# One weight load is requested four steps later: behind the write of the tenth tile of tokens

## The chip, the cores and the metric

The kernel runs on one core of a Trainium2 chip. Its engines are TensorE (PE in the profile, with its weight loads as PEld), VectorE (DVE), ScalarE (ACT), GpSimd (POOL) and SyncE (SP), which here does nothing but issue transfers. All transfers of SP stand in one queue that 16 DMA engines serve; GpSimd's gathers and scatters stand in a queue of their own, on the same 16 engines. The metric is the device time of one execution in microseconds: 433.91 us is the median of three runs before the change (433.2 to 435.3).

## What is computed

Three stages on 2 x 768 = 1536 tokens of 512 numbers. First an attention with decaying state for 8 heads, then a gated feed-forward stage with a convolution along the sequence, and then a mixture of 8 experts in which each token goes to one expert:

```python
def _moe_ref(x, w_in, conv_w, w_out):
    h = np.maximum(x @ w_in, 0.0)
    ...
    return (h * gate @ w_out).astype(np.float32)

def _moe2_ref(x, w_gate, w_local, w1, w2):
    logits = np.einsum('bsd,de->bse', x, w_gate)
    ...
            fresh_e = int(np.argmax(logits[b, s]))
            if s == 0 or local_gate[b, s] < 0.5:
                e = fresh_e
            else:
                e = prev_e if prev_e >= 0 else fresh_e
            ...
            h = np.maximum(x[b, s] @ w1[e], 0.0)
            out[b, s] = p[e] * (h @ w2[e])
```

Everything is float32. The change touches only the passage from the second stage to the third.

## The kernel before, in words

The tokens are cut into 12 tiles of 128, six for each of the two sequences. For each tile, `ffn_out` multiplies the gated hidden values with `w_out` on TensorE (L133 to L135, three matmuls for each product, tile `x_ps`). ScalarE copies the finished tile to SBUF (L486) and SP writes it to a DRAM buffer `xs` (L488), 256 KB for each tile. Tiles 1 to 10 go through a buffer `xn`; the last two (`xl4`, `xl5`) stay in SBUF as well, because the first two expert tiles take their rows from there.

While the second sequence's tiles are made, routing on VectorE works out which token goes to which expert, and writes a table `ei` of experts (L619) and a table `it` of token numbers (L657).

The third stage works on 11 expert tiles of 128 tokens that share an expert, and on two groups of smaller quarter tiles. For expert tile j, `gather(j)` zeroes a buffer `xg` and lets GpSimd fetch the tile's tokens from `xs` by an indirect DMA (L724). The gathers of tiles 0 and 1 need the first ten writes to `xs`; their rows from the last two tiles are added on TensorE from SBUF (`begin_x`, `late_x`, L810 and L816). The third gather is that of the first quarter group (number 16). It and all later ones need all twelve writes. TensorE turns a gathered tile (L797, `tp<-cs,xg`) and then multiplies it with w1 (tile `g`) and w2 (tile `y`). ScalarE and VectorE cut the weights in a high and a low part first (`cut`, L714 and L715).

Weights come in 2 MB pieces, each as four transfers of 512 KB that SP issues: `fetch(j, which)` (L695, buffers `r`; which is 0 for w1 and 1 for w2) for expert tile j, and `fetch_q` (L705, buffers `qc` and `qs1l`) for the quarter groups. From the second expert tile on (`fetch(1, ...)`) SP reads the expert's number from `ei` before it issues (L676).

There is no scheduler: every engine executes its instructions in the order in which the code issues them. For the second sequence this order is set by the loop at L769. Its step n is one call of `ffn_out` (six matmuls), and the tiles are written at n = 2, 4, 8, 12, 16 and 20. Tables, weight requests and gathers are put in at given values of n; `experts` follows with `fetch(1, 1)`, `fetch_q(0, 0, 1)`, the turning of tiles 0 and 1, and gather 16.

Of the kernel before, what the change touches and what calls it, by code (L numbers as in the profile page):

```python
# [91 lines left out]
def tile_kernel(ctx, tc, cat, cst, qT, kT, kN, vN, w_in, conv_w, w_out, wg, w1, w2, out):  # L92
# [378 lines left out]
    def ffn_out(b, t, ms):  # L471

        ts = slice(t * P, (t + 1) * P)
        if ms[0] == 0:
            OUT[b, t] = psb.tile([P, DM], F32, tag="x2", name="x2_ps")
        ps = OUT[b, t]
        for m in ms:
            g = hg[b, m]
            mm3(ps, g[:, 0, ts], g[:, 1, ts], wo_hi[:, m, :], wo_lo[:, m, :], m == 0, m == 7)
        if ms[-1] == 7:  # L480
            if b == B - 1 and t >= NG - 2:
                xn = xpool[0].tile([P, DM], F32, name=f"xl{t}", bufs=1)
                LAST.append(xn)
            else:
                xn = rt.tile([P, DM], F32, name="xn", bufs=2)
            se.activation(out=xn, in_=OUT.pop((b, t)), func=AF.Copy)  # L486
            r = b * S + t * P
            sy.dma_start(out=xs[r:r + P, :], in_=xn)  # L488
# [194 lines left out]
    def fetch(j, which):  # L683

        src = (w1, w2)[which].rearrange("e p a n -> e p (a n)")
        kw = {}
        if j == 0:
            src = src[0]
        else:
            src = src[bass.ds(expert_at(j), 1)].rearrange("o p n -> (o p) n")  # L690
            if j > 1:
                kw = dict(cond=sy.value_load(ei[0:1, 1, j:j + 1], min_val=0, max_val=1), cond_hint=True)
        dst = raw(j % 2, which)
        for i in range(4):
            sy.dma_start(out=dst[:, i, :], in_=src[:, i * 1024:(i + 1) * 1024], **kw)  # L695

    def fetch_q(g, which, i):

        tag = QSLOT[nq[0] % 2]
        nq[0] += 1  # L700
        QW[g, which, i] = w = home(tag).tile([P, 4, 1024], F32, tag=tag, name="q" + tag)
        src = (w1, w2)[which].rearrange("e p a n -> e p (a n)")
        for u in range(4):
            one_e = src[bass.ds(expert_at(NTILE + 4 * g + u), 1)].rearrange("o p n -> (o p) n")
            sy.dma_start(out=w[:, u, :], in_=one_e[:, i * 1024:(i + 1) * 1024])  # L705

    def cut(j, which, i):

        tag = SLOT[ncut[0] % len(SLOT)]
        ncut[0] += 1  # L710
        w = home(tag).tile([P, 2, 2, 1024], F32R, tag=tag, name="w" + tag)
        for h in range(2):
            r = RAW[j % 2, which][:, 2 * i + h, :]
            se.activation(out=w[:, 0, h, :], in_=r, func=AF.Copy)  # L714
            ve.tensor_tensor(out=w[:, 1, h, :], in0=r, in1=w[:, 0, h, :].bitcast(F32), op=ALU.subtract)  # L715
        W[j, which, i] = w.rearrange("p s h n -> p s (h n)")
# [3 lines left out]
    def gather(j, n=NT):  # L720

        X[j] = xg = xpool[0].tile([P, DM], F32, name="xg")
        po.memset(xg, 0.0)
        return po.indirect_dma_start(out=xg, out_offset=None, in_=xs[0:n], in_offset=bass.IndirectOffsetOnAxis(ap=it[:, j:j + 1], axis=0),  # L724
                                     bounds_check=n - 1, oob_is_err=False)
# [43 lines left out]
    for n, (t, ms) in enumerate(units, 1):  # L769
        ffn_out(1, t, ms)  # L770
        for step in STEPS.get(n, ()):
            next(step, done)
        if n == 8:
            fetch(1, 0)
        if n in (10, 14):
            cut(0, 0, n // 14)
        if n == 13:
            fetch_q(0, 0, 0)
            for j in range(2):
                gather(j, NT - 2 * P)  # L780
# [279 lines left out]
```

## Time and profile before

| what | us |
|---|---|
| median of three runs (lowest to highest) | 433.91 (433.2 to 435.3) |
| the profiled execution | 433.53 |
| its span, first to last instruction | 431.8 |
| PE busy | 406.7 (94%) |
| DVE busy | 290.1 (67%) |
| ACT busy | 259.4 (60%) |

Times in the profile count from the start of the span, so that an event at 240.02 us is 240.02 us after the first instruction. The 1.7 us between the profiled execution and its span lie around the program. The profile gives the granted clock of TensorE as a share of full speed; it is 1.00 in all of the stretches shown below. An idle time in brackets behind an instruction is that of its engine just before it, with what ended it.

### The profile page before, as it was taken

To read this page: it belongs to the slowest core of one execution; us is meant where nothing else is said; L and a number is where in the kernel's file an instruction comes from. 1 tells how busy PE (TensorE), PEld (TensorE's weight loads), DVE (VectorE), ACT (ScalarE), POOL (GpSimd) and SP (SyncE) were. 2 spreads that over 40 slices of the span, in tenths; PEclk is the share of its full clock that TensorE was granted. 3 is DMA by queue.
4 is the path that set the end of the run, shared out by engine and by line. 5 is a ranking of instruction groups with operands and counts; after the bars stand their busy time and mean duration, and the time that the engine had idled before them with its cause. 6 is when DMAs were issued, how large, how long until landed. Compare 5 with 4: busy or idle time off the path is not lost.

```text
span 431.8 us, 7294 instructions
## 1 busy us (share of the span) xinstructions
PE 406.7 (94%) x2412; PEld 327.2 (76%) x2412; DVE 290.1 (67%) x518; ACT 259.4 (60%) x429; POOL 91.6 (21%) x92
## 2 busy tenths in 40 slices
PE   8898999997999999999999899999989999999991
PEld 7787897896898778989768676867738676776881
DVE  3798789798766350477899057968663796858650
ACT  2787677666755212566604166869555786958560
POOL 5256664213000000000000330205212132111210
PEclk9999999999999999999999999999999999999997
DMA  7989773320000101000296999999979999675001
GB/s 239 380 289 399 257 218 87 96 92 1 2 2 0 49 29 46 26 0 2 82 355 214 358 382 350 347 385 407 379 272 330 393 367 362 266 257 205 34 26 37
DMA packets 27324, 86.59 MB, mean 201 GB/s; under 512 B 3598, under 2 KB 4622, under 8 KB 27280
## 3 DMA queue, kind: packets, MB, share of 16 engines
q1 hardware_dynamic: 25200, 79.76, 50.6%
q0 software_dynamic: 2080, 6.29, 3.8%
q8 instruction: 21, 0.34, 0.3%
q14 instruction: 23, 0.19, 0.1%
HBM read 105.18 MB, written 6.55 MB: 259 GB/s over the span
## 4 chain that ended last, share of the span: by engine, by line
PE 35%; issue 26%; DMA 18%; DVE 14%; ACT 3%; POOL 2%; SPq 0%; POOLq 0%; DVEq 0%
DMA out_dram<-yo,it 15%; PE h_ps L133 5%; PE h_ps L135 4%; PE h_ps L134 4%; PE x_ps L133 4%; PE x_ps L134 3%; PE x_ps L135 3%; PE y L297 3%; PE s_ps L279 3%; DVE cc L350 2%; DMA kv<-in_kN_dram 2%; DVE na L149 2%; PE inc L287 2%; DVE na L150 1%; PE y L299 1%
## 5 line engine op out<-in xcount | busy, mean ns | idle before, releaser
L133 PE MATMUL h_ps<-xT,wih 128*128 128x384 f32 x128 | 46.5, 363 | 2.3 <-ACT wc L192 2.3
L350 DVE SCALAR_TENSOR_TENSOR cc<-h,cw,cc 128x768 f32<-128x768 f32 x32 | 35.1, 1097 | 16.8 <-ACT cc L347 16.8
L860 POOL DMA_INDIRECT out_dram<-yo,it x13 | 16.7, 1283 | 137.1 <-ACT yo L859 137.1
L724 POOL DMA_INDIRECT xg<-xs,it x13 | 18.8, 1442 | 125.5 <-DMA qc<-in_w_dram 118.6
L134 PE MATMUL h_ps<-xT,wih 128*128 128x384 f32 x128 | 43.1, 337 | 0.0
L135 PE MATMUL h_ps<-xT,wil 128*128 128x384 f32 x128 | 43.1, 336 | 0.0
L133 PE MATMUL x_ps<-woh,hg 128*128 128x512 f32 x96 | 38.5, 401 | 0.0
L134 PE MATMUL x_ps<-wol,hg 128*128 128x512 f32 x96 | 37.5, 391 | 0.0
L135 PE MATMUL x_ps<-woh,hg 128*128 128x512 f32 x96 | 37.5, 390 | 0.0
L715 DVE TENSOR_TENSOR ws0l<-r,ws0l 128x1024 fp32r<-128x1024 f32 x22 | 26.0, 1222 | 16.3 <-ACT ws0l L714 16.1
L297 PE MATMUL y<-at,vz 128*128 128x128 f32 x192 | 30.6, 281 | 1.7 <-DMA kv<-in_kN_dram 0.9
L715 DVE TENSOR_TENSOR ws0h<-r,ws0h 128x1024 fp32r<-128x1024 f32 x22 | 26.0, 1222 | 8.3 <-ACT ws0h L714 8.2
L715 DVE TENSOR_TENSOR wc<-r,wc 128x1024 fp32r<-128x1024 f32 x22 | 25.9, 1221 | 7.9 <-ACT wc L714 7.9
L714 ACT ACTIVATE ws0l<-r 128x1024 fp32r<-128x1024 f32 x22 | 22.1, 1052 | 13.6 <-PE y L135 13.6
L153 POOL TENSOR_TENSOR na<-na,raw 128x512 int32<-128x512 int32 (+1 forms) x17 | 21.9, 1290 | 38.2 <-DVE na L150 12.6
L715 DVE TENSOR_TENSOR ws1h<-r,ws1h 128x1024 fp32r<-128x1024 f32 x22 | 26.0, 1222 | 6.0 <-ACT ws1h L714 4.0
L279 PE MATMUL s_ps<-qz,kq 128*128 128x256 f32 x96 | 29.0, 384 | 1.0 <-DVE qz L248 1.0
L714 ACT ACTIVATE wc<-r 128x1024 fp32r<-128x1024 f32 x22 | 22.1, 1054 | 11.3 <-PE g L135 11.3
L297 PEld LDWEIGHTS y<-at,vz 128*128 128x128 f32 x192 | 25.3, 191 | 4.3 <-DVE xT L302 2.3
L133 PEld LDWEIGHTS h_ps<-xT,wih 128*128 128x128 f32 x128 | 24.1, 188 | 5.5 <-ACT wc L192 2.6
L281 DVE TENSOR_TENSOR at<-s_ps,ca 128x256 f32<-128x256 f32 x48 | 20.2, 420 | 11.6 <-PE s_ps L279 11.5
L486 ACT ACTIVATE xn<-x_ps 128x512 f32<-128x512 f32 x10 | 6.0, 599 | 32.8 <-PE x_ps L135 15.5
(231 smaller groups left out, 1041.5 us busy)
## 6 DMA issues: line engine op xcount, KB each, us to landing
r<-in_w_dram SPq DMA_DIRECT2D x88, 512.0 KB
qc<-in_w_dram SPq DMA_DIRECT2D x32, 512.0 KB
qs1l<-in_w_dram SPq DMA_DIRECT2D x32, 512.0 KB
raw<-in_w_in_dram SPq DMA_DIRECT2D x8, 512.0 KB
raw<-in_w_out_dram SPq DMA_DIRECT2D x8, 512.0 KB
kq<-in_qT_dram SPq DMA_DIRECT2D x7, 384.0 KB
kq<-in_kT_dram SPq DMA_DIRECT2D x7, 384.0 KB
kv<-in_vN_dram SPq DMA_DIRECT2D x7, 384.0 KB
```

The source lines that it names most:

```text
L133: te.matmul(ps, lhi, rhi, start=first, stop=False)
L134: te.matmul(ps, lhi, rlo, start=False, stop=False)
L135: te.matmul(ps, llo, rhi, start=False, stop=last)
L153: po.tensor_tensor(out=a, in0=a, in1=lo, op=ALU.add)
L279: te.matmul(ps, self.kq[:, 0, tok], self.qz[:, :, tok], start=True, stop=True)
L281: ve.tensor_tensor(out=self.at[c], in0=ps, in1=self.dm, op=ALU.mult)
L297: te.matmul(y, vz[:, c, j, :], at[:, j, :], start=(j == 0), stop=(c == 0 and j == 1))
L350: ve.scalar_tensor_tensor(out=cc, in0=h[:, i:i + S], scalar=cw[:, m, i:i + 1], in1=cc, op0=ALU.mult, op1=ALU.add)
L714: se.activation(out=w[:, 0, h, :], in_=r, func=AF.Copy)
L715: ve.tensor_tensor(out=w[:, 1, h, :], in0=r, in1=w[:, 0, h, :].bitcast(F32), op=ALU.subtract)
L724: return po.indirect_dma_start(out=xg, out_offset=None, in_=xs[0:n], in_offset=bass.IndirectOffsetOnAxis(ap=it[:, j:j + 1], axis=0), bound ...
L860: po.indirect_dma_start(out=out, out_offset=bass.IndirectOffsetOnAxis(ap=it[:, j:j + 1], axis=0), in_=yo, in_offset=None, bounds_check=NT ...
```

## The change

The request for w1 of the second expert tile (`fetch(1, 0)`, four transfers of 512 KB into buffer `r10`) moves from step n = 8 of the loop to n = 12.

```diff
         ffn_out(1, t, ms)
         for step in STEPS.get(n, ()):
             next(step, done)
-        if n == 8:
+        if n == 12:
             fetch(1, 0)
         if n in (10, 14):
             cut(0, 0, n // 14)
         if n == 13:
             fetch_q(0, 0, 0)
             for j in range(2):
                 gather(j, NT - 2 * P)
```

On SP, before the change, the four transfers of `r10` (with the reading of the expert's number) stand between the write of the ninth tile (`xn_2290`) and that of the tenth (`xn_2368`); `qc4` is the first weight piece of the quarter group:

```order
L488 DMA xs_65<-xn_2290 128x512
L676 TENSOR_LOAD ei_1515
L676 ISA x2
L695 ISA
L695 DMA r10_2127<-in_w1_dram 128x1024
...
L488 DMA xs_65<-xn_2368 128x512
L676 TENSOR_LOAD ei_1515
L676 ISA x2
L705 ISA
L705 DMA qc4_2404<-in_w1_dram 128x1024
```

On SP, after it, at the same place (the tenth tile's write is now `xn_2355`):

```order
L488 DMA xs_65<-xn_2290 128x512
L488 DMA xs_65<-xn_2355 128x512
L676 TENSOR_LOAD ei_1515
L676 ISA x2
L695 ISA
L695 DMA r10_2127<-in_w1_dram 128x1024
...
L676 TENSOR_LOAD ei_1515
L676 ISA x2
L705 ISA
L705 DMA qc4_2404<-in_w1_dram 128x1024
```

The write has moved ahead of the four transfers, and nothing else on SP has moved. Behind `qc4` follow, in both, the writes of `xl4` and `xl5` and then w2 of the second expert tile. The other four engines have the same instructions in the same order in both kernels; on GpSimd, for one, the gathers of tile 0 (`xg_2445`), tile 1 (`xg_2450`) and quarter group 16 (`xg_2619`) stand like this in both:

```order
L723 MEMSET xg_2445 128x512
L724 DMA xg_2445<-xs_65,it_1513 128x512
L723 MEMSET xg_2450 128x512
L724 DMA xg_2450<-xs_65,it_1513 128x512
L723 MEMSET xg_2619 128x512
L724 DMA xg_2619<-xs_65,it_1513 128x512
```

## Rows read from the trace of the kernel before

**Rows 1.** Waits of PE, 215 to 290 us: in total, times, longest.
```profile
PE tp L810 <- DMA xg<-xs,it: 2.0, 1, 2.0
...
PE g L133 <- ACT hr L848: 0.7, 1, 0.7
```

**Rows 2.** Timeline of PE: start, duration, line, tile, count, idle time before.
```profile
243.19 0.39 PE L135 MATMUL x_ps<-woh,hg 128*128 128x512 f32 x1
245.58 1.13 PE L810 MATMUL tp<-cs,xg 128*128 128x128 f32 x8 [2.00 <-DMA xg<-xs,it]
...
247.44 1.06 PE L810 MATMUL tp<-cs,xg 128*128 128x128 f32 x8
...
256.82 0.60 PE L797 MATMUL tp<-cs,xg 128*128 128x128 f32 x4
258.16 0.50 PE L133 MATMUL g<-ws1h,xh 128*128 128x512 f32 x1 [0.74 <-ACT hr L848]
```

**Rows 3.** Timeline of POOL: the gathers of tiles 0, 1 and 16.
```profile
240.02 1.21 POOL L724 DMA_INDIRECT xg<-xs,it  x1 [118.57 <-DMA qc<-in_w_dram]
...
242.05 1.01 POOL L724 DMA_INDIRECT xg<-xs,it  x1 [0.28 <-POOL xg L723]
...
247.52 1.00 POOL L724 DMA_INDIRECT xg<-xs,it  x1 [3.91 <-DMA xs<-xl]
```

**Rows 4.** Timeline of DVE: the table of token numbers.
```profile
234.16 0.18 DVE L657 SCALAR_TENSOR_TENSOR it<-pl,pv 128x20 uint32<-128x20 f32 x1
```

**Rows 5.** Timeline of SP: when the transfers are issued.
```profile
228.62 0.32 SPq L488 DMA_DIRECT2D xs<-xn  x1
230.05 1.95 SPq L695 DMA_DIRECT2D r<-in_w_dram  x4
232.11 0.55 SPq L488 DMA_DIRECT2D xs<-xn  x1
233.46 4.05 SPq L705 DMA_DIRECT2D qc<-in_w_dram  x4
...
245.40 2.17 SPq L695 DMA_DIRECT2D r<-in_w_dram  x4
```

**Rows 6.** Stretches: busy time by engine (PE, PEld, DVE, ACT, POOL), clock, DMA share, GB/s.
```profile
226.00:228.00 2.00, 2.00 (x11) 1.64 (x10) 1.83 (x12) 0.00 (x0) 0.00 (x0) 1.00 0.05 13
230.00:232.00 2.00, 2.00 (x10) 1.67 (x9) 1.93 (x9) 1.12 (x3) 0.00 (x0) 1.00 0.42 98
232.00:244.00 12.00, 11.58 (x57) 9.41 (x55) 5.62 (x12) 2.84 (x4) 3.30 (x4) 1.00 1.01 384
244.00:246.00 2.00, 0.42 (x4) 0.45 (x5) 0.00 (x0) 0.21 (x1) 0.00 (x0) 1.00 0.95 366
246.00:248.00 2.00, 2.00 (x20) 2.00 (x19) 0.00 (x0) 0.00 (x0) 0.48 (x1) 1.00 0.78 177
```

**Rows 7.** Chain that ended last, 228 to 262 us: the twelfth tile's write.
```profile
244.24 2.51 DMA xs<-xl
```

**Rows 8.** Gathers, issue on POOL to landing: the one that starts at 247.52 alone.
```profile
DMA to landing us min/median/max: 7.6/7.6/7.6
```

**Rows 9.** Timeline of ACT.
```profile
228.00 0.60 ACT L486 ACTIVATE xn<-x_ps 128x512 f32<-128x512 f32 x1 [9.79 <-DMA xs<-xn]
...
231.37 0.60 ACT L486 ACTIVATE xn<-x_ps 128x512 f32<-128x512 f32 x1 [0.88 <-ACT ws0h L714]
...
257.02 1.09 ACT L848 ACTIVATE hr<-g 128x512 f32<-128x512 f32 x2 [1.42 <-PE g L135]
```

**Rows 10.** Gathers, issue on POOL to landing: all 13 of the trace.
```profile
DMA to landing us min/median/max: 4.0/7.2/8.4
```

**Rows 11.** The same for the last one (377.99 us), with few transfers beside it.
```profile
DMA to landing us min/median/max: 4.6/4.6/4.6
```

**Rows 12.** Waits of SP, 228 to 300 us.
```profile
SPq L705 <- PE hq_ps L889: 1.9, 2, 1.5
```

**Rows 13.** Waits of PEld, 270 to 330 us.
```profile
PEld yq_ps L911 <- DMA qs1l<-in_w_dram: 3.3, 3, 2.0
```

## The prediction

> **What bounds the kernel now.** I first read the stretches and the waits of PE around the place of the change, then the timelines of the five engines there, and last how long the gathers take to land.
>
> PE is busy for 94% of the span, so time is won or lost here only where PE stands still. The list of its waits between 215 and 290 us shows two such places that matter: 2.0 us in front of `tp` L810 for a gather, and 0.7 us in front of `g` L133 for ScalarE [rows 1]. The timeline shows them in place. PE's last `x_ps` matmul ends at 243.19 + 0.39 = 243.58, and the first expert tile's turning starts at 245.58, released by gather 0 [rows 2]. Gather 0 itself started at 240.02, after GpSimd had stood still for 118.57 us [rows 3]. What held it? It needs the table `it` and the first ten writes. The table was written at 234.16 + 0.18 = 234.34 [rows 4]. The tenth write was issued at 232.11, but behind 2 MB of `r10` issued from 230.05 on, in the same queue [rows 5]. The profile puts the wait down to a `qc` transfer, which the gather doesn't need; I read that as a name drawn from shared semaphores, since of what the gather does need only the tenth write can be that late. The queue is full: 1.01 of the DMA engines' time and 384 GB/s from 232 to 244 us [rows 6]. At that rate 2 MB take 2.10 MB / 384 GB/s = 5.5 us.
>
> The second thing to see is what follows. The twelfth write is issued at 244.24 and lands 2.51 us later, at 246.75 [rows 7]; just then the queue is running dry, 366 and then 177 GB/s [rows 6]. Gather 16, which needs that write, starts 0.77 us behind it, at 247.52 [rows 3], and lands 7.6 us later, at 255.1 [rows 8]. PE turns its tile at 256.82 [rows 2]. So there are 1.7 us to spare there.
>
> **The change, part by part.**
>
> The tenth write no longer waits. ScalarE is done with its tile at 231.37 + 0.60 = 231.97 [rows 9], SP has nothing else to do, and the queue is nearly empty (98 GB/s from 230 to 232 us, and most of that will be gone) [rows 6]. With the 2.51 us of the twelfth write [rows 7] it lands at 234.5, and with GpSimd's 0.77 us gather 0 starts at 235.3, after the table. The landing takes between 4.0 and 8.4 us over all gathers [rows 10]; I take the median, 7.2, which gives 242.5, with 239.3 and 243.7 as bounds. Gather 1 follows 2.03 us after gather 0, as now [rows 3], and lands at 244.5; PE comes to it 1.86 us after it began [rows 2], at 245.4. Both gathers are there in time. PE's wait goes: -2.0 us, with 1.9 at the worse bound.
>
> `r10` and all that is queued behind it come later. Before, SP needed 230.05 - 228.94 = 1.1 us from the end of a write's issue to the first transfer of `r10` (the expert's number is read in between) [rows 5]. Now it starts from 232.0 + 0.3, so `r10` goes out at 233.4 instead of 230.05: 3.4 us later. The tenth write, 0.26 MB or 0.7 us at 384 GB/s, no longer stands between `r10` and `qc`. So `qc` and what is behind it move back by 2.7 us. Of `r10` itself nobody is short: at 384 GB/s its 2 MB are through some 8 us after 233.4, the 2.5 us of a transfer's own time included, and the first matmul that needs them is `g` at 258.16 [rows 2]. The quarter group's `qc` is needed later still.
>
> The victim is the twelfth write. It is still issued at 244.24, since that hangs on PE's last `x_ps`, but now into a queue that is 2.7 us behind: it lands at 246.75 + 2.7 = 249.4. The bounds are 246.75, if the queue should have caught up, and 250.2, if the whole 3.4 us stay. Gather 16 then starts at 249.4 + 0.77 = 250.2. For its landing I have 7.6 from its own row [rows 8], and 7.2 as the median of all 13 [rows 10]; I take 7.4, so 257.6. Its bounds are 4.6, what the last gather needed with little beside it [rows 11], and 8.4.
>
> PE now comes to gather 16's tile at 256.82 - 2.0 = 254.8 and waits 2.8 us for it, to 257.6. The turning takes 0.6 us, so the next matmul, `g` of the second tile, starts at 258.2. Before, it started at 258.16, because PE had stood there 0.74 us for ScalarE's `hr` (257.02 + 1.09 = 258.11) [rows 2, 9]. That wait is gone, since `hr` is done 2 us earlier, at 256.1, while PE waits for the gather. Sum at this place: 258.2 - 258.16, or 0.0 us. The 2.0 us won at 245 us are given back at 257: the gather lands 2.5 us later and PE comes 2.0 us earlier, 4.5 together; less the 1.7 that were to spare this is the new wait of 2.8, and less the 0.7 that goes behind it, 2.1.
>
> [...] The rows say that a gather beside a full queue took 7.6 us, and one with little beside it 4.6 [rows 8, 11]. [...]
>
> Behind 258 us I cost the rest at nothing. The weights `qs1l` are asked for behind `qc` and the gathers. What the queue lacked at 246 to 248 us, 2 us x (1 - 177/384) = 1.1 us, is now used, so of the 2.7 us at most 1.6 are left for them. No wait for `qs1l` stands in the list up to 290 us [rows 1]; if that cover were gone, it would cost up to 1.6 us. Later requests for `qc` wait for PE (1.9 us in two waits) [rows 12], so the transfers follow PE, and the stall of 3.3 us in front of `yq_ps` [rows 13] moves with it and neither absorbs nor adds.
>
> The sum is against the profiled execution: 431.8 us of span and 1.7 us around it make 433.53, plus 0.0. That execution is 0.4 us under the median of the three runs, so I forecast 433.9 for the median.
>
> **The rivals.**
>
> *The gain stays.* Gather 16 lands in time after all, because the DMA engines take its rows in between the weights (4.6 us from 250.2: 254.8), or because the queue has caught up by 244 us (write at 246.75). Then PE goes on from 254.8 through the turning, waits for `hr` to 256.1, and `g` starts 2.0 us earlier: 431.9. For it speaks the row of 4.6 us; against it, that 4.6 was measured with an almost idle queue, and that the median of all is 7.2 [rows 10].
>
> *The twelfth write trails.* This is the side on which the kernel gets slower. The write into `xs` whose landing released ScalarE at 228.00 [rows 9] stood behind eight weight transfers, and between 226 and 228 us the DMA engines moved just 13 GB/s, 0.05 of their time [rows 6]: the stream was through, and one engine's rest of a write still came 2 us later. In the changed kernel the twelfth write stands behind eight weight transfers too. If one engine trails by 2 us there, it lands at 251.4, gather 16 at 259.6, and `g` starts at 260.2: +2.0, or 435.9. Beyond 0.5% it goes if the write lands later than 251.6. Against it: the tenth write before, behind four transfers, landed at 240.02 - 0.77 = 239.3 if gather 0 followed it as gather 16 followed the twelfth, within about 1 us of what the stream from 232 us says (5.5 and 0.7 us, so 238.2).
>
> *The tenth write wasn't it.* If gather 0 had waited for `qc` after all, as the profile names it, it would not start at 235 us but later than now, by up to the 2.7 us of the queue. PE would wait at L810 as before or longer, and the third term would stay: 434 to 436. Against it stands the order of the program: nothing in the gather reads `qc`.
>
> **How the numbers follow.** The forecast gets 0.60, the gain that stays 0.17, the trailing write 0.18, the wait for something else 0.05. 0.5% is 2.2 us, about what a measurement of this kernel can tell from no change. The full gain of 2.0 us lies just inside, so a third of that case and a little of the forecast's scatter count as faster: 0.08. Of the trailing write a good half counts as slower, with a bit from the last case and from the 1.6 us of `qs1l`: 0.13. The rest, 0.79, is within. The range goes from 431.9, the gain in full, to 436.0, the trailing write: 8 in 10 or a little more.
>
> **What would show it.** Right would be: gather 0 starts at about 235 us, PE goes from `x_ps` to L810 without the 2.0 us, the twelfth write takes about 5 us instead of 2.51, gather 16 starts at about 250 us, a new wait of PE for `xg` of 2 to 3 us in front of the turning L797, and no wait for `hr` behind it. Wrong in the second half if gather 16's start stays near 247.5 us, or if no wait stands in front of that L797; wrong in the first if gather 0 still starts near 240 us.

## The result: half a per cent slower, and where the time went

The changed kernel took 436.11 us (median of 13 executions, 434.4 to 441.1 apart from one of 814.6), the kernel before 433.91 (13 executions beside them, 431.1 to 435.9). The ratio is 1.0058 with a 95% interval of [1.0034, 1.0082]; a second measurement of the same two kernels gave 436.60 against 433.48, ratio 1.0057 [1.0027, 1.0087]. (A ratio is estimated from the executions side by side and need not be the quotient of the two medians.) The forecast was 433.9, no change. It was wrong: the time lies just outside the range, on the slower side.

The first profile of the changed kernel fell in an execution of 441.09 us, in which TensorE's clock had been at half for 3.4 us from 14.5 us on and for 6.8 us from 106.7 us on, long before the change. At the place of the change it shows the same two things as the second profile, a wait of 4.61 us at L797 and 3.4 us at half clock behind it. The profile of the second measurement is shown here: 435.82 us, span 434.1, mean granted clock 0.987. Up to PE's last `x_ps` matmul, which the change does not touch, this execution is already 0.76 us later than the profiled one before (243.95 against 243.19, [rows 2]); times below are compared with this shift taken off.

The shift is the clock's as well. Near 104 us PE stands idle for 2.3 us in every profile here. Up to 102 us this execution is level with the one before (0.07 us ahead); behind the idle stretch its clock was at half from 105.3 to 108.7 us, and from 116 us on it is 0.76 us late. PE in the kernel before, then in the changed one, and then the stretch 106 to 108 us of both in the same order (PE, PEld, DVE, ACT, POOL busy; granted clock, DMA share, GB/s):

```profile
105.91 0.44 PE L133 MATMUL h_ps<-xT,wih 128*128 128x384 f32 x1 [2.31 <-ACT wc L192]
```

```profile
105.84 0.69 PE L133 MATMUL h_ps<-xT,wih 128*128 128x384 f32 x1 [2.32 <-ACT wc L192]
```

```profile
106.00:108.00 2.00, 2.00 (x12) 2.00 (x13) 1.69 (x4) 2.00 (x5) 0.81 (x1) 1.00 0.00 0
```

```profile
106.00:108.00 2.00, 2.00 (x7) 2.00 (x8) 1.71 (x4) 2.00 (x5) 0.88 (x1) 0.50 0.00 0
```

Of the fourteen profiles that this document rests on, seven have such a fall behind 104 us and seven do not, with the code up to there the same in all.

The waits of PE from 215 to 290 us, as in [rows 1] (in total, times, longest):

```profile
PE tp L797 <- DMA xg<-xs,it: 3.5, 1, 3.5
```

The two waits of before, 2.0 us at L810 and 0.7 us for `hr` (the hidden values of the first expert tile, which ScalarE writes), are gone, and one of 3.5 us has come. In the timeline of PE (start, duration, line, tile, count, idle time before; compare [rows 2]):

```profile
243.95 0.40 PE L135 MATMUL x_ps<-woh,hg 128*128 128x512 f32 x1
244.19 1.05 PE L810 MATMUL tp<-cs,xg 128*128 128x128 f32 x8
...
255.12 0.39 PE L135 MATMUL g<-ws0l,xl 128*128 128x512 f32 x1
259.05 1.11 PE L797 MATMUL tp<-cs,xg 128*128 128x128 f32 x4 [3.54 <-DMA xg<-xs,it]
259.82 0.77 PE L133 MATMUL g<-ws1h,xh 128*128 128x512 f32 x1
260.39 0.63 PE L134 MATMUL g<-ws1h,xh 128*128 128x512 f32 x1
...
262.42 0.40 PE L133 MATMUL g<-ws1h,xh 128*128 128x512 f32 x1
```

L810 follows `x_ps` at once: the first half of the forecast came true. Then comes the wait at L797, and behind it something that was not forecast: the same matmuls take 0.63 us instead of 0.39, until 262.4. The stretches show why (PE, PEld, DVE, ACT, POOL busy; granted clock, DMA share, GB/s):

```profile
256.00:258.00 2.00, 0.00 (x0) 0.00 (x0) 0.00 (x0) 0.64 (x2) 1.26 (x2) 1.00 1.01 394
258.00:259.00 1.00, 0.00 (x0) 0.00 (x0) 0.00 (x0) 0.00 (x0) 0.00 (x0) 0.94 1.04 410
259.00:262.00 3.00, 2.95 (x9) 2.56 (x10) 0.22 (x1) 1.80 (x3) 0.00 (x0) 0.50 1.02 390
263.00:265.00 2.00, 2.00 (x17) 1.54 (x19) 1.14 (x2) 0.57 (x2) 0.00 (x0) 1.00 0.77 285
```

While PE stood idle the granted clock fell from 1.00 to 0.50 of full speed, just before 259 us, and PE worked at half clock from 259 until a little past 262 us. In the kernel before, PE had stood idle for 2.00 us in front of L810 with no fall behind it [rows 2, 6].

What PE waited for: the gathers on GpSimd (compare [rows 3]), then the landing of the twelfth write in the chain that ended last (compare [rows 7]), then gather 16 from issue to landing (compare [rows 8]):

```profile
235.96 1.21 POOL L724 DMA_INDIRECT xg<-xs,it  x1 [113.76 <-DVE pr L662]
...
252.45 1.00 POOL L724 DMA_INDIRECT xg<-xs,it  x1 [12.57 <-DMA xs<-xl]
```

```profile
245.01 6.67 DMA xs<-xl
```

```profile
xg<-xs,it POOLq DMA_INDIRECT x1, 6.6
```

Gather 0 starts at 235.96, 4.8 us earlier than before, released by VectorE (L662, just behind the table) and no longer by a transfer. The twelfth write takes 6.67 us instead of 2.51, and gather 16 starts 4.2 us later than before.

Where PE stands against the profiled execution before, from the starts of the same instructions with the last `x_ps` as zero (minus is earlier; `hq_ps` and `yq_ps` are the products of a quarter group with w1 and w2):

| place | forecast | changed kernel |
|---|---|---|
| L810, first expert tile | -2.0 | -2.16 |
| L797, gather 16's tile | +0.8 | +1.47 |
| first `g` of the second expert tile | 0.0 | +0.90 |
| first `hq_ps` | 0.0 | +2.02 |
| last matmul of group 16's `yq_ps` | 0.0 | +0.99 |
| end of the span | 0.0 | +1.53 |

### The profile page after: what moved, and what is told of

Read it like the earlier page. It is cut to its first block, busy times and chain, and to the rows that moved or that the text cites. A ratio compares the mean times of both kernels' runs of the same rounds, so it can differ in the third digit from the quotient of the medians.

```text
span 439.3 us, 7294 instructions
## 1 busy us (share of the span) xinstructions
PE 412.3 (94%) x2412; PEld 332.4 (76%) x2412; DVE 290.4 (66%) x518; ACT 259.8 (59%) x429; POOL 93.4 (21%) x92
## 4 chain that ended last, share of the span: by engine, by line
PE 36%; issue 25%; DMA 19%; DVE 13%; ACT 3%; POOL 2%; SPq 0%; POOLq 0%; DVEq 0%; ACTq 0%
DMA out_dram<-yo,it 15%; PE h_ps L133 5%; PE h_ps L134 4%; PE h_ps L135 4%; PE x_ps L133 4%; PE x_ps L134 3%; PE x_ps L135 3%; PE y L297 3%; PE s_ps L279 3%; DVE cc L350 2%; DMA kv<-in_kN_dram 2%; DMA xs<-xl 2%; DVE na L149 2%; PE inc L287 1%; PE y L299 1%
## 5 line engine op out<-in xcount | busy, mean ns | idle before, releaser
L133 PE MATMUL h_ps<-xT,wih 128*128 128x384 f32 x128 | 47.8, 373 | 2.3 <-ACT wc L192 2.3
L724 POOL DMA_INDIRECT xg<-xs,it x13 | 20.5, 1579 | 129.5 <-DVE pr L662 113.8
L134 PE MATMUL h_ps<-xT,wih 128*128 128x384 f32 x128 | 44.2, 346 | 0.0
L135 PE MATMUL h_ps<-xT,wil 128*128 128x384 f32 x128 | 44.2, 345 | 0.0
L133 PEld LDWEIGHTS h_ps<-xT,wih 128*128 128x128 f32 x128 | 25.1, 196 | 5.5 <-ACT wc L192 2.6
L301 ACT ACTIVATE xT<-y 128x128 fp32r<-128x128 f32 x48 | 13.2, 274 | 21.2 <-PE y L299 19.3
```

The costliest lines, as they stand in the source:

```text
L133: te.matmul(ps, lhi, rhi, start=first, stop=False)
L134: te.matmul(ps, lhi, rlo, start=False, stop=False)
L135: te.matmul(ps, llo, rhi, start=False, stop=last)
```

## Experiments

Theory A is the forecast's mechanism with the new price: the loss is made at L797, by gather 16's wait for the late twelfth write, and by the half clock behind that wait. Theory B is that the weights as a whole are later, and the loss would be made elsewhere anyway. Each kernel was timed beside the kernel before on the same chip.

### Gather 16 without the twelfth write

```diff
-        gather(NTILE)
+        gather(NTILE, NT - 2 * P)
```

> The changed kernel, but gather 16 reads only the first ten tiles of tokens (the quarter group's rows from the last two tiles are left out), so it no longer needs the twelfth write. Theory A (the loss is the twelfth write, stuck behind r10 and qc, which starts gather 16 late; PE then waits 4.6 us at L797 and runs 3.4 us at half clock after it): gather 16 starts near 239 us, no wait at L797, no drop of the clock, and the 2.0 us won at L810 stay: 431.9 us, 4 us under the changed kernel. Rival B (the loss is in the weights, since r10, qc and qs1l land later and their readers wait): the wait moves to the first reader of qs1l, and the time stays near 436.

Measured: 433.87 us against 433.87, ratio 0.9983 [0.9953, 1.0014], against 1.0058 for the change as it stands. PE's timeline has no wait at L797, and the matmuls behind it take 0.40 us, as at full clock:

```profile
254.77 0.60 PE L797 MATMUL tp<-cs,xg 128*128 128x128 f32 x4
256.10 0.50 PE L133 MATMUL g<-ws1h,xh 128*128 128x512 f32 x1 [0.74 <-ACT hr L848]
```

So the whole loss hangs on gather 16's need for the last two writes: that part of theory A is shown. But the gain of 2 us that should then appear in the time did not. PE was 2.2 us ahead up to 263 us and 1.7 us up to 317; then PEld's waits (270 to 330 us) show

```profile
PEld yq_ps L911 <- DMA qs1l<-in_w_dram: 4.5, 4, 1.1
...
PEld yq_ps L911 <- DMA qc<-in_w_dram: 1.0, 1, 1.0
```

instead of 3.3 us [rows 13], and behind them PE was level with the kernel before.

### One of the two weight requests behind the twelfth write

```diff
-        if n == 12:
+        if n == 20:
             fetch(1, 0)
```

> r10 is requested behind the twelfth write (n = 20) instead of the tenth's. Theory A: both writes go ahead of r10; the twelfth stands behind qc alone, which is through by about 241 us, and lands near 246.5; gather 16 starts near 247 and lands at 254 to 255, when PE comes to it; -2.0 to -0.5 us against before (431.9 to 433.4), the upper end if r10 or qs1l, now 3 us later on SP, are waited for. Rival B: r10 comes 12 us later than in the changed kernel and is waited for, so slower than it: 437 or more.

Measured: 437.78 us, ratio 1.0093 [1.0061, 1.0125]. L797 has no wait, but `r10` is now late for ScalarE, whose cut of it stands ahead of `hr` in its order:

```profile
257.45 0.65 PE L797 MATMUL tp<-cs,xg 128*128 128x128 f32 x4
262.00 0.80 PE L133 MATMUL g<-ws1h,xh 128*128 128x512 f32 x1 [3.90 <-ACT hr L848]
```

Behind this wait of 3.9 us the clock is at half again, over twice the time (a stretch in the middle of it):

```profile
264.00:266.00 2.00, 2.00 (x6) 1.53 (x5) 1.78 (x2) 0.33 (x1) 0.00 (x0) 0.50 1.02 410
```

The other request was moved instead in the next kernel (`r10` stays as in the change):

```diff
+        if n == 20:
+            fetch_q(0, 0, 0)
         if n == 13:
-            fetch_q(0, 0, 0)
             for j in range(2):
                 gather(j, NT - 2 * P)
```

> The changed kernel with the first quarter piece qc requested behind the twelfth write (n = 20) instead of at n = 13. Theory A: the eleventh and twelfth writes have only r10 ahead of them, the twelfth lands near 246.5, no wait at L797; qc and qs1l go out 4 us later on SP and may cost up to 2 us at the first matmuls of the quarter group: 432 to 434. Rival B: the later qc is the worse for it: 437 or more, with the wait at L889.

Measured: 438.91 us, ratio 1.0114 [1.0081, 1.0148]. No wait at L797 here either; the quarter group's second piece now comes too late, so that PE waits four times, 2.4 us together, the first time here:

```profile
264.43 1.04 PE L890 MATMUL hq_ps<-qs1l,xq 128*32 128x512 f32 x2 [1.73 <-DMA qs1l<-in_w_dram]
```

Either 2 MB taken from in front of the twelfth write removes the wait at L797 (the write then takes 2.05 and 2.46 us): the write waits for the two together. And either one, moved behind that write, is missed elsewhere at once. Of theory A the landing came true in both kernels, of rival B the time.

### TensorE kept busy during the wait

Sixteen matmuls of the identity with itself, on a tile that is overwritten later, fill the wait in front of L797 of the changed kernel (in the profile each stands as two records). The tile is taken ahead of them for that.

```diff
+        h = psq.tile([P, 2, 512], F32, tag="q", name="hq_ps")
+        if g == 0:
+            for _ in range(16):
+                te.matmul(h[:, 0, 0:P], ident, ident, start=True, stop=True, skip_group_check=True)
         ps = turn(X.pop(NTILE + g), 0)
...
-        h = psq.tile([P, 2, 512], F32, tag="q", name="hq_ps")
```

> The changed kernel with 16 small matmuls (128x128, into the group's PSUM tile that is written anew behind them) on PE just before it turns gather 16's tile: some 3.6 us of work in the wait of 4.6 us. Theory A: the wait shrinks to about 1 us, gather 16 lands as before, the clock stays at full speed behind it, and the 1.6 us that the half clock costs are gone: 434.5. If the half clock has nothing to do with the wait: it is still there, and the time stays near 436.

In the profile the half clock is gone (granted clock 1.00 from 256 to 264 us):

```profile
255.79 0.39 PE L135 MATMUL g<-ws0l,xl 128*128 128x512 f32 x1
256.01 3.73 PE L882 MATMUL hq_ps<-cs 128*128 128x128 f32 x32
259.68 0.66 PE L797 MATMUL tp<-cs,xg 128*128 128x128 f32 x4
260.09 0.48 PE L133 MATMUL g<-ws1h,xh 128*128 128x512 f32 x1
260.40 0.40 PE L134 MATMUL g<-ws1h,xh 128*128 128x512 f32 x1
```

The matmuls behind L797 take 0.40 us instead of 0.63, and PE reaches `hq_ps` 0.45 us late instead of 2.02. So in the profile the half clock costs some 1.5 us. The time followed by less: 435.93 us, ratio 1.0033 [1.0001, 1.0065] against 1.0057 [1.0027, 1.0087]. The medians differ by 0.7 us or less where 1.6 were expected, by the ratios it is 1.0 us, and the intervals overlap: the timed size of this term is unclear.

The mean clocks of the timed executions say that the half clock itself is not a thing of single profiles. In the profiles, an execution without half clock inside the program has a mean of 0.992 to 0.994, one with a single stretch of 3.4 us 0.989 to 0.991. Of 93 timed executions of the kernel before, 23 have 0.993 or more; of 23 of the changed kernel none has, and of the 12 with the busy wait 4 have (those of 438.8, 441.1 and 814.6 us are left out). The means are 0.990, 0.987 and 0.991. So the busy wait took the half clock out of the timed executions too; why the time did not follow is not shown.

### The twelfth write late by itself

The kernel before, with only the write of `xl5` issued behind w2 of the second expert tile.

```diff
+        HOLD[1, 5]()
```

(The line stands behind `fetch(1, 1)`; L488 keeps the write of that tile in `HOLD` instead of issuing it.)

> The kernel before, with one row of SP moved: the twelfth write stands behind the four transfers of r11 (w2 of the second expert tile) instead of ahead of them. Nothing else moves and no byte is added. Theory A (a late twelfth write is the whole loss): it lands about 5.3 us later (2 MB at 384 GB/s), gather 16 lands near 260.4 instead of 255.1, PE waits 3 to 5 us at L797 and then runs a few us at half clock; the wait of 2.0 us at L810 stays: +2.9 us at the next matmul, +4.5 with the clock, 436.8 to 438.4. Rival B (the late weights are the loss): r11 is even earlier, so 433.9.

Measured: 436.45 us, ratio 1.0079 [1.0050, 1.0107], a loss as theory A wants it, but made in another place. SP no longer waits for ScalarE with the write, so `fetch(1, 1)` went out at 240.76 instead of 245.40 [rows 5]:

```profile
238.68 0.33 SPq L488 DMA_DIRECT2D xs<-xl  x1
240.76 1.92 SPq L699 DMA_DIRECT2D r<-in_w_dram  x4
244.12 0.33 SPq L488 DMA_DIRECT2D xs<-xl  x1
```

These 2 MB ran beside gather 0. PE waited longer for gather 0, and its clock fell:

```profile
243.08 0.39 PE L135 MATMUL x_ps<-woh,hg 128*128 128x512 f32 x1
246.79 1.14 PE L814 MATMUL tp<-cs,xg 128*128 128x128 f32 x8 [3.33 <-DMA xg<-xs,it]
247.76 1.89 PE L820 MATMUL tp<-oh,xl 128*128 128x128 f32 x8
```

```profile
249.00:250.00 1.00, 1.00 (x7) 1.00 (x6) 0.00 (x0) 0.00 (x0) 0.00 (x0) 0.50 1.00 397
```

The wait alone cost 1.3 us against before, the half clock another 1.65 (PE is 2.97 late at the turning of gather 16's tile). At that tile it waited for nothing, since it came late itself. The test of the write failed, because its issue was also what held `fetch(1, 1)` back; what it did show is the half clock once more, at another place, behind a wait of 3.3 us.

### The other way: `r10` ahead of the ninth write

The kernel before, with the ninth tile's write held back and issued behind `fetch(1, 0)`; the second kernel also has a third buffer `xn`.

```diff
         if n == 8:
             fetch(1, 0)
+            HOLD[1, 2]()
```

> The kernel before, with r10 requested just ahead of the ninth write instead of just behind it: the other way from the change. r10 then goes out at about 227.5 instead of 230.05, into a queue that stands empty from 226 to 230 us. Theory A, with the transfers up to 321 us as a second bound: the tenth write and all behind it land 2.5 us earlier, gather 0 starts near 237.5, the wait at L810 goes, the twelfth write stays near 246.5, and the stall at yq_ps does not grow, since the stream is as far ahead as PE: -2.0 us, 431.9. If the stall at yq_ps gives everything back as in the run with gather 16 freed: 433.9.

> As the run before (r10 ahead of the ninth write), and with three buffers xn instead of two, so that ScalarE's copy of the ninth tile no longer waits for the write of the seventh (idle 9.79 us before 228.00). The ninth and tenth writes are ready earlier; r10 hangs on the table ei (226.4) alone and goes out at about 227.3. Theory A: as the run before or 0.2 to 0.5 us better, 431.5 to 431.9; if the copy's wait had cost nothing, exactly as the run before.

Measured: 433.59 us, ratio 1.0000 [0.9970, 1.0029], and 433.24, ratio 1.0004 [0.9971, 1.0037]. In both profiles PE's wait at L810 was 0.5 to 0.6 us and PE some 1.4 us ahead from there on, to the end of the span (1.4 and 1.5 us), so that the stall at `yq_ps` did not give it back either. Yet the times are those of before, and theory A's 431.9 did not come. This made me doubt the 2.0 us of [rows 1] as a typical value; the controls below bear on it. The changed kernel itself was measured again with these:

> The changed kernel once more, beside the others on this chip: 436.1 us by its first measurement. Theory A: a wait of 3 to 5 us at L797 for gather 16, and a few us at half clock behind it; the twelfth write's last DMA engine 1.5 to 2 us behind the middle one. If the half clock came from that one disturbed execution alone, it is missing here.

Its result and profile are those shown above.

### The stall at `yq_ps` taken away, and a control

For the third and fourth piece of w2 of quarter group 16, the first and second are used again, 4 MB fewer; three kernels have this edit: the one before, the changed one, and the changed one with gather 16 on the first ten tiles. The fourth is the kernel before with gather 16 on the first ten tiles.

```diff
+        if (g, which) == (0, 1) and i > 1:
+            QW[g, which, i] = KEEP[i - 2]
+            return
         tag = QSLOT[nq[0] % 2]
...
```

(`KEEP` holds each piece as it is fetched; its lines are left out here.)

> The kernel before, with two weight pieces of 2 MB fewer: for the third and fourth piece of w2 of quarter group 16 the first and second are read again (part of that group's result is left out so). These two pieces are what PE waits for in front of yq_ps at 317 to 324 us (3.3 us in the kernel before). Theory A (that stall is a bound of its own, set by the stream of weights): about 3 us faster than before, 430.5 to 431.5. Theory B (the stream is late as a whole, and the next stall takes over): 433 or more. It is the base for the next two runs.

> The changed kernel with the same two pieces fewer. Theory A: PE is some 2 us behind the base up to 316 us (1.5 to 3, longer wait at L797 and half clock behind it) and, with no stall in front of yq_ps to take some of it back, stays so to the end: 1.5 to 3 us above e9_before_short_stall. Theory B (the loss comes from the queue, not from the place at 259 us): within 1 us of it.

> The changed kernel with gather 16 reading only the first ten tiles (as e1_gather16_first_ten, the rows of the last two tiles left out of the quarter group) and the same two pieces fewer. Theory A: PE keeps its 2.2 us from 245 us on, past 324 us to the end: 1.7 to 2.3 us under e9_before_short_stall, where e1 lost them in front of yq_ps. Theory B: the gain is lost to another wait for weights, within 0.7 us of e9.

> Control for e1: the kernel before with gather 16 reading only the first ten tiles (the rows of the last two left out of the quarter group). Gather 16 then starts about 244 us instead of 247.5, where PE had 1.7 us to spare. Theory A: nothing else hangs on it, 433.5 to 434.2, same as before. Rival: fewer rows or an earlier gather are worth something by themselves: 432 to 433, and part of what e1 showed is theirs.

| kernel | us | ratio to before (434.32) |
|---|---|---|
| before, short stall | 429.99 | 0.9914 [0.9884, 0.9943] |
| change, short stall | 433.58 | 0.9982 [0.9958, 1.0007] |
| change, first ten, short stall | 430.11 | 0.9915 [0.9882, 0.9948] |
| before, first ten | 433.74 | 1.0007 [0.9978, 1.0036] |

The stall is a bound of its own: without it the kernel before is 4.3 us faster (3 expected). Without it the change costs 3.6 us by the medians and 3.0 by the ratios, about theory A's upper end, and theory B's "within 1 us" is out. PE's timeline has the wait and the half clock (granted 0.50 from 261 to 263 us) as in the changed kernel:

```profile
259.64 0.76 PE L800 MATMUL tp<-cs,xg 128*128 128x128 f32 x4 [3.34 <-DMA xg<-xs,it]
260.06 0.78 PE L133 MATMUL g<-ws1h,xh 128*128 128x512 f32 x1
260.63 0.63 PE L134 MATMUL g<-ws1h,xh 128*128 128x512 f32 x1
```

Counted as in the table of places, PE is at +1.30 at the turning, +0.38 at `g` and +1.93 at `hq_ps`, and holds +1.93 up to 317 us, where its own base, the kernel before with the short stall, is at -0.89. But theory A failed on the third kernel: 1.7 to 2.3 us under the first were expected, and 0.1 above was measured. The profile of its base shows one reason. In that kernel nothing is changed up to 300 us, and still PE waited only 0.52 us at its L810 (L813 there, by three lines added above it); in the control, equally unchanged up to there, 1.62:

```profile
244.36 0.39 PE L135 MATMUL x_ps<-woh,hg 128*128 128x512 f32 x1
245.27 1.13 PE L813 MATMUL tp<-cs,xg 128*128 128x128 f32 x8 [0.52 <-DMA xg<-xs,it]
```

```profile
243.42 0.39 PE L135 MATMUL x_ps<-woh,hg 128*128 128x512 f32 x1
245.43 1.13 PE L810 MATMUL tp<-cs,xg 128*128 128x128 f32 x8 [1.62 <-DMA xg<-xs,it]
```

So the wait that the change removes is 0.5, 1.6 or 2.0 us from one execution of the same code to the next, by how the transfers stand to PE when it arrives. Two things differ in the three. The last part of the seventh tile's write, whose buffer ScalarE needs for the ninth, landed at 227.16, 227.56 and 227.90, and gather 0 started at 239.49, 239.88 and 240.02 (in the order of the waits). And in the first of them PE came 1.17 us later than in the kernel before, 1.0 of it from half clock at 106 us. Against the 0.5 of its base the third kernel gained 0.7 at L810, and gave 0.55 back at `hq_ps<-qs1l`, whose sixteen matmul records took 3.00 us there and 2.44 in the base:

```profile
261.52 3.00 PE L892 MATMUL hq_ps<-qs1l,xq 128*32 128x512 f32 x16
```

```profile
263.47 2.44 PE L892 MATMUL hq_ps<-qs1l,xq 128*32 128x512 f32 x16
```

The control is the same as before, so gather 16's earlier start and fewer rows are worth nothing by themselves that these measurements can tell.

## Why the prediction was wrong, step by step

**The tenth write goes free: right in the changed kernel, over-valued in the base.** Gather 0 started at 235.96 - 0.76 = 235.2 (forecast 235.3), and PE came to L810 2.16 us earlier (2.0). That the two starts agree is luck in part: the tenth write had landed at 234.0 already (2.00 us after its issue, not 2.51), and the gather started with the end of VectorE's L662 (235.79 + 0.17, or 235.2 with the shift taken off), which the forecast did not have. The rival that the gather really waited for `qc` is out: GpSimd's releaser is now VectorE, and the first `qc` is issued only at 236.94. But the 2.0 us were read from one execution. Three profiles of that passage unchanged have 2.0, 1.6 and 0.5; against the middle one the gain was about 1.8, and no kernel here showed it in its time, not even the two in which gather 16 had nothing to wait for.

**The twelfth write: the step that was mis-sized.** It was put at 249.4, 5.2 us after its issue, by the 2.7 us that the queue is behind. In the six profiles with the change's order on SP it took 6.4 to 7.2 us (6.67 in the one shown). Within it, the middle one of its 16 parts landed at 249.68 - 0.76 = 248.9 in the changed kernel, earlier than forecast, and the last 2.0 us later, at 250.9 (1.4 to 2.1 us in the six, 0.3 in the kernel before). That is the rival "the twelfth write trails", which had 0.18. That its time, 435.9, comes close to the measured one is luck: it had the gather 0.8 us too slow and no half clock. I had priced the stream and not the last part of the write. And it was the last that counted: gather 16 started 0.77 us behind it (252.45, and the write's end at 245.01 + 6.67 = 251.68), the same 0.77 us as in the kernel before.

**Gather 16: a little better than forecast.** 6.6 us instead of 7.4. Of the write's 1.5 us this gives back 0.8, so PE's wait was 3.3 to 3.5 us instead of 2.8, and `g` stood at +0.4 to +0.9 instead of 0.0. Of the +0.9 some 0.4 is the clock's already: from the turning to `g` it took 0.77 us in the changed kernel, at half clock, and 0.42 where the clock fell later (short stall). The 4.6 us that the prediction's rival had for it did not come: beside a full queue (1.01 of the DMA engines' time and 394 GB/s from 256 to 258 us) gather 16 took 6.6 and, with the short stall, 6.7 us. That the engines take its rows in between the weights was a supposition, and no run shows it.

**The clock: the step that was left out.** I let PE go on at full speed behind the new wait, because all shown stretches of before were at 1.00 and the idle 2.0 us at L810 had no price. Behind the 3.5 us (and 3.3 with the short stall) came 3.4 us at half clock: 0.4 us ahead of `g` and 1.1 behind it, and 1.55 behind it with the short stall. This is the larger of the two terms, 1.5 against some 0.5 us, and together they turned a forecast of 0.0 into +2.0 at `hq_ps`. The busy wait, +0.45 there with the same late write, shows that it is the idling and not the write alone. Its timed size stays open; an estimate is 1.3 us, from the 0.0036 by which the mean clock of the changed kernel's executions lies under that of the kernel before, and the 1.4 us that go with each 0.004 among the executions of the kernel before.

**Behind 258 us: one sentence goes too far.** That the stall in front of `yq_ps` "neither absorbs nor adds" does not hold to the size of the terms here. Over it, PE's place against the profiled kernel before changed by +1.7 us in the first experiment and by -1.0 in the changed kernel, whose wait for `qs1l` was 2.4 us instead of 3.3 [rows 13]:

```profile
PEld yq_ps L911 <- DMA qs1l<-in_w_dram: 2.4, 2, 1.2
```

But it changed by -1.0 in the control too, which came there 0.35 us early, and by only +0.1 in the kernel with `r10` ahead of the ninth write, which came there 1.5 us early. So what the stall takes or gives varies by 1 us and more between profiles, and that it takes from whoever arrives early is not shown. With it taken away the change costs 3.6 us by the medians instead of 2.2 to 3.1, which is not clear of the noise.

**The sum.** -2.16 at L810, +3.06 from there to `g` (forecast 2.0; 0.4 of it half clock), +1.12 half clock behind `g`, -1.03 at `yq_ps` and +0.54 behind it make the +1.53 at the end of the changed kernel's span; with the 0.76 us of shift, 434.1 - 431.8 = 2.3 us, where the medians say 2.2 and 3.1. That agreement is luck in part, since the shift is the half clock behind 104 us, which has nothing to do with the change. At `hq_ps` the changed kernel is 2.0, 2.4 and 3.4 us behind the three profiles of the unchanged passage. What stays open is why the busy wait gained so little in the time, and how the wait at L810 is spread over many executions: only three profiles of it unchanged exist.

No kernel here beat the one before with all of the work done.

## What to carry to other kernels

A wait that a change moves is not worth the same at its new place: ask how long TensorE will stand idle in one piece there, because here two waits of 2.0 and 0.7 us cost just themselves, and waits of 3.3 and 3.5 us cost a third to a half as much again behind them. A shorter wait is not safe from that: behind the one of 2.3 us near 104 us seven of fourteen executions lost 0.8 to 2.3 us at half clock. Before two profiles are compared, it pays to see in each where the clock was at half. A small transfer that others wait for, queued behind megabytes of weights, has to be priced by its last part, which here landed 2.0 us behind the middle one where it had been 0.3 in the kernel before. And a wait of 2 us that is read from one profile should be looked for in a second one before a forecast counts all of it as gain.

## What was not expected of the hardware

The granted clock fell at each single idle stretch of 3.3, 3.5, 3.9 and 4.6 us that TensorE had in these profiles, and not at one of 2.0 us in the same part of the program; at the one of 2.3 us near 104 us it fell in seven profiles of fourteen. At those of 3.5 and 3.9 us it fell before the wait was over; at the one of 3.3 us in front of L814 it fell 1.0 us after TensorE had begun to work again, and at the other of 3.3 and the one of 4.6 us 0.4 and 0.5 us after. Half clock lasted 3.4 us at those of 3.3, 3.5 and 4.6 us, and about 6.8 us at the one of 3.9, so it did not grow with the wait. The twelfth write's parts landed within 0.6 us of each other when little was queued ahead of it (246.15 to 246.75 in the kernel before), and within 1.8 to 2.8 us of each other behind 4 MB of weights (248.64 to 251.42 in the kernel with gather 16 on the first ten tiles and the short stall).
